# A bank for the first q: attention and two gated layers on one Trainium2 core

## The chip, the core and the metric

The kernel runs on one core of one Trainium2 chip. The metric is device time in microseconds for one launch. The core has a matrix engine (TensorE, PE in the rows, with its weight loads as PEld), a vector engine (VectorE, DVE), a scalar engine (ScalarE, ACT), GpSimd (POOL) and SyncE (SP), which issues most DMAs. Matmuls write into PSUM, which this kernel divides into eight banks of 512 float32 columns.

## The reference

What is computed, cut to what matters: attention over 4 batches, 8 heads, 576 positions and 64 dimensions, in which scores more than tau below their row's maximum are dropped, and behind it two layers with 512 inputs and 2048 hidden values for each of the 2304 tokens.

```python
scores = scale * q @ k.T
thresh = max(scores, axis=-1) - tau
scores = where(scores >= thresh, scores, -1e9)
attn = softmax(scores)            # divided by (sum + 1e-9)
x = (attn @ v), heads side by side, 2304 x 512
h = x @ moe_w_in;  x = (h * clip(h + 3, 0, 6) / 6) @ moe_w_out
h = x @ moe2_w_in; x = (h - tanh(h)) @ moe2_w_out
```

## The kernel before

**Staging.** The work is written as tasks. Each task names its engine, an assumed duration, a key, and the buffers that it reads and writes. Nothing is issued while the tasks are recorded: at the end `plan.issue()` runs a list scheduler over all of them. At each moment, each engine takes, of the tasks whose inputs are ready, the one with the lowest key. The order that comes out is the order in which instructions stand on each engine, so a task that becomes ready at another moment can change the order of all that follows. The chip then runs each engine's instructions in that order, each waiting for its data.

**Buffers.** A `Ring` has n places. For a ring with `free=True`, a task that writes a new buffer can be taken only when one of the places is free, which it is when all users of its last buffer have ended. `R_tp` (L350) is the ring of transposes: two PSUM banks. `R_m` (L397) is layer 1's ring: two banks, too, made for the products of the first layer. One of the two is taken at the start (L980) as `unread`, into which fill-in matmuls write that nobody reads (`filler`, L683): 24 calls' worth before anything else, and further ones wherever PE's planned busy share over the planner's look-back falls under `SHARE`, until the first tokens have been scaled. The other serves the weights of layer 1 in the beginning: `load_w` gets `scratch=R_m` (L1089, L1099), and three VectorE steps (L447, L450, L453) pass each weight through it.

**Attention.** `units` are (batch, half of the rows, pair of heads, head, chunk of 128 rows). For each pair, the rounds come first. `k_round` transposes the keys: part 0 is four PE transposes of the main rows, part 1 two of the left-over 64 rows (L606). Each takes a buffer of `R_tp`; ScalarE copies it (L613) as the high part and VectorE subtracts the high part (L615), which gives the low part, so that the scores can be formed with two products. `q_round` does the same for q: GpSimd doubles the loaded rows (L583), PE makes four transposes (L590), ScalarE copies with the scale (L620) and VectorE subtracts (L622). `v_round` takes a buffer of `R_tp` for a column sum (L657) from which v's scale is made. `softmax` then has PE make the scores (L712), VectorE the maximum (L717), ScalarE the exponential (L719), VectorE the threshold (L728); ScalarE and GpSimd split the result (L733, L739), a DMA transposes it (L742), and `weighted` multiplies it with v (L765).

**Order at the start.** The rounds of a pair have the key `when(u)` of a unit some places ahead: keys six and five units ahead (`LK`), q four (`LQ`), v two (`LV`), with `when(u) = T0 + STEP * u + SLOW * min(u, KNEE)`, T0 8.4, STEP 3.03 and SLOW 0.8. The first pair's first unit is 0, the second pair's is 4. The first q is loaded from ScalarE's queue, all others from SP's. Layer 1 begins when its weights and the first tokens are scaled, and is then interleaved with the attention; the second layer follows, with PE as its bound.

Of the kernel before, what the change touches and what calls it, by code (L numbers as in the profile page):

```python
# [73 lines left out]
class Plan:  # L74
# [13 lines left out]
    def add(self, eng, dur, key, fn, r=(), w=(), after=(), xfer=0.0, hold=False, slack=0.0, port=None):  # L88
        r, w = ([getattr(b, "of", b) for b in x] for x in (r, w))
        deps = dict.fromkeys(after)  # L90
        for b in r:
            deps.update(dict.fromkeys(b.writers))
        t = Task(eng, dur, key, fn, deps, xfer, hold, slack, eng == "pool" if port is None else port)
        t.w = w
        users = dict.fromkeys((*r, *w))
        t.free = [b for b in users if b.ring.free]
        for b in users:
            b.users.append(t)
        for b in w:
            b.writers.append(t)  # L100
        self.tasks.append(t)
        return t
# [110 lines left out]
def attention_moe_moe_kernel(  # L213
# [131 lines left out]
    def at_ring(*a):  # L345
        at_rings.append(ring(*a))
        return at_rings[-1]

    R_s = at_ring(ps_s, 2, [128, 2, 512], F32, "s")
    R_tp = Ring(2, lambda i: ps_t.tile([128, 512], F32, tag=f"tp{i}", name="tp"), free=True)  # L350
# [15 lines left out]
    R_q = at_ring(at_p, 2, [128, 2, 2, 256], F32R, "q")  # L366
# [30 lines left out]
    R_m = Ring(2, lambda i: ps_m.tile([128, 512], F32, tag=f"m{i}", name="m"), free=True)  # L397
# [144 lines left out]
    KR, QR, VR, KL, QL, KS, VT, SV, QT = ({} for _ in range(9))  # L542
# [42 lines left out]
    def transposes(ps, srcs):  # L585

        o = 0
        for s, p0 in srcs:
            w = s.shape[0]
            nc.tensor.transpose(ps[:, o:o + w], s.rearrange("p r d -> p (r d)"), ident[p0:p0 + w, p0:p0 + w])  # L590
            o += w
# [26 lines left out]
    def q_split(qt, tp, out, n, key):  # L618
        src = lambda: tp.t[:, 0:2 * n].rearrange("p (i n) -> p i n", i=2)
        hi = add("act", t_act(2 * n, scalars=True), key + RK, lambda: nc.scalar.activation(  # L620
            out=out(0), in_=src(), func=ACTF.Copy, scale=tau_b[:, 2:3]), r=[tp], w=[qt])
        add("dve", t_dve(2 * n, scalars=True), key + RK, lambda: nc.vector.scalar_tensor_tensor(  # L622
            out=out(1), in0=src(), scalar=tau_b[:, 2:3], in1=out(0).bitcast(F32), op0=ALU.mult, op1=ALU.subtract),
            r=[tp], w=[qt], after=[hi])

    def q_round(b, g, j, key):

        qr, tp, qt = QR[b, g, j], R_tp.new(), R_q.new()
        add("pe", 4 * 0.11, key, lambda: transposes(
            tp.t, [(qr.t[:, i, c, :, :], 0) for i in range(2) for c in range(2)]), r=[qr], w=[tp, qt])  # L630
        q_split(qt, tp, lambda x: qt.t[:, x], 256, key)
        QT[b, g, j] = qt
# [335 lines left out]
    with tc.manual_schedule():  # L968
# [94 lines left out]
        def record_round(r, key):  # L1063
            kind = r[0]
            if kind == "k":
                _, b, j, part = r
                if part == 0:
                    load_k(b, j, key - LD * STEP)
                    if j == 0:
                        load_k_left(b, key - LD * STEP)  # L1070
                k_round(b, j, part, key)
            elif kind == "q":
                _, b, g, j = r
                if g == 1 and 2 * j % NP == 0:
                    load_q_left(b, 2 * j // NP, key - LD * STEP)
                load_q(b, g, j, key - LD * STEP, "act" if (b, g, j) == (0, 0, 0) else "dma")
                q_round(b, g, j, key)
            elif kind == "l":
                q_left_round(r[1], r[2], key)
            elif kind == "v":  # L1080
                load_v(*r[1:], key - LD * STEP)
                v_round(*r[1:], key)
# [410 lines left out]
        for idx, st in enumerate(order2):  # L1493
# [72 lines left out]
            else:  # L1566
                a, b = R_m.new(), R_m.new()
# [55 lines left out]
```

## Time and profile before

| | us |
|---|---|
| median of 3 runs | 1069.54 |
| lowest and highest | 1065.81, 1070.72 |
| the profiled execution | 1068.02 |
| its span in the profile | 1066.2 |
| PE, DVE, ACT, POOL busy | 1011.5, 804.5, 725.0, 362.6 |

The span runs from the first to the last instruction in the profile of one execution. The busy time of PE includes the fill-in matmuls, and the ends of matmuls are modelled. PEclk is the share of TensorE's full clock that was granted; its two levels are 1.2 and 2.4 GHz. "idle before <-releaser" is the time for which an engine stood still before an instruction, and what ended it.

### The profile page before, as it was taken

To read this page: it belongs to the slowest core of one execution; us is meant where nothing else is said; L and a number is where in the kernel's file an instruction comes from. 1 tells how busy PE (TensorE), PEld (TensorE's weight loads), DVE (VectorE), ACT (ScalarE), POOL (GpSimd) and SP (SyncE) were. 2 spreads that over 40 slices of the span, in tenths; PEclk is the share of its full clock that TensorE was granted. 3 is DMA by queue.
4 is the path that set the end of the run, shared out by engine and by line. 5 is a ranking of instruction groups with operands and counts; after the bars stand their busy time and mean duration, and the time that the engine had idled before them with its cause. 6 is when DMAs were issued, how large, how long until landed. Compare 5 with 4: busy or idle time off the path is not lost.

```text
span 1066.2 us, 23814 instructions
## 1 busy us (share of the span) xinstructions
PE 1011.5 (95%) x9202; PEld 775.5 (73%) x9202; DVE 804.5 (75%) x1627; ACT 725.0 (68%) x1345; POOL 362.6 (34%) x385
## 2 busy tenths in 40 slices
PE   7776987899999999999999999999999999999997
PEld 5676776679888778988886778776576666666664
DVE  5999898969887578777457896389976887774573
ACT  7876979889888687877456783468655774664332
POOL 3666667777577455666210000000001111211000
PEclk9999996999999999999999999999999999999999
DMA  7999897767898675876558774143335765664235
GB/s 187 187 228 231 160 228 189 165 133 148 172 189 150 136 147 126 150 160 119 99 163 290 232 210 135 45 150 104 102 122 146 181 140 107 131 118 61 79 108 129
DMA packets 284948, 161.47 MB, mean 151 GB/s; under 512 B 203171, under 2 KB 261027, under 8 KB 284835
## 3 DMA queue, kind: packets, MB, share of 16 engines
q1 hardware_dynamic: 279024, 150.25, 58.1%
q0 software_dynamic: 5184, 9.44, 6.6%
q8 instruction: 72, 1.18, 0.5%
q10 hardware_dynamic: 624, 0.26, 0.1%
q14 instruction: 44, 0.34, 0.1%
HBM read 76.02 MB, written 41.42 MB: 110 GB/s over the span
## 4 chain that ended last, share of the span: by engine, by line
PE 75%; DVE 9%; ACT 7%; DMA 5%; issue 2%; SPq 1%; POOL 0%; DVEq 0%; ACTq 0%; POOLq 0%
PE m L517 22%; PE ya L517 21%; PE h L517 9%; PE m L959 8%; PE s L712 6%; PE tp L765 5%; PE tp L590 2%; DVE e L728 2%; ACT e L719 1%; DVE z L717 1%; DMA pt<-pp 1%; DMA xT<-xs 1%; PE m L686 1%; DVE m L450 1%; ACT pp L733 1%
## 5 line engine op out<-in xcount | busy, mean ns | idle before, releaser
L517 PEld LDWEIGHTS <-wo 128*128 128x128 f16 x2112 | 201.3, 98 | 58.7 <-DVE wo L453 2.2
L739 POOL TENSOR_TENSOR pp<-e,pp 128x128 f16<-128x128 f32 (+3 forms) x156 | 180.5, 1176 | 110.9 <-ACT pp L733 58.8
L517 PE MATMUL ya<-wo,g 128*128 128x512 f16 x864 | 205.4, 379 | 2.5 <-ACT g L879 1.1
L517 PEld LDWEIGHTS <-wi 128*128 128x128 f16 x1536 | 150.0, 98 | 39.3
L517 PE MATMUL m<-xT,wo 128*128 128x256 f16 (+1 forms) x1248 | 170.4, 285 | 2.9 <-DVE wo L453 1.9
L1443 POOL DMA_DIRECT2D po<-o x36 | 31.3, 876 | 410.9 <-ACT o L1437 410.9
L517 PEld LDWEIGHTS <-g 128*128 128x128 f16 x864 | 83.7, 98 | 82.1 <-DVE g L883 3.1
L728 DVE SCALAR_TENSOR_TENSOR e<-s,z,e 128x576 f32<-128x576 f32 x144 | 116.5, 812 | 26.7 <-ACT e L719 23.7
L717 DVE TENSOR_REDUCE z<-s 128x1 f32<-128x576 f32 x144 | 107.4, 750 | 35.4 <-PE s L712 34.4
L959 PE MATMUL m<-g,wo 128*128 128x256 f16 (+1 forms) x960 | 130.8, 284 | 0.7 <-DVE t L873 0.7
L712 PE MATMUL s<-ks,q 128*128 128x288 f32 x512 | 102.3, 324 | 21.9 <-DVE e L728 21.3
L879 ACT ACTIVATE g<-t 128x512 f16<-128x512 f32 (+1 forms) x168 | 94.3, 565 | 37.5 <-DVE t L1410 24.7
L719 ACT ACTIVATE e<-s,z 128x576 f32<-128x576 f32 x144 | 105.0, 737 | 21.8 <-DVE z L717 20.5
L959 PEld LDWEIGHTS <-wo 128*128 128x128 f16 x960 | 88.9, 98 | 21.8 <-DVE t L873 1.0
L712 PEld LDWEIGHTS s<-ks,q 128*128 128x128 f32 x512 | 75.5, 195 | 31.1 <-DVE e L728 13.8
L517 PE MATMUL m<-x,wi 128*128 128x256 f16 x768 | 94.9, 273 | 0.0
L1408 ACT ACTIVATE t<-t,hid_s 128x512 f32<-128x512 f32 x72 | 51.6, 718 | 62.7 <-DVE t L1399 62.2
L733 ACT ACTIVATE pp<-e 128x1152 f16<-128x1152 f32 (+1 forms) x80 | 85.0, 1063 | 12.9 <-DVE e L728 9.9
L765 PE MATMUL tp<-vt,pt 128*128 128x65 f16 (+1 forms) x2240 | 84.2, 196 | 5.6 <-DMA pt<-pp 1.9
L765 PEld LDWEIGHTS <-pt 128*128 128x128 f16 (+1 forms) x2240 | 79.0, 102 | 13.8 <-issue 7.6
L517 PE MATMUL ya<-g,wo 128*128 128x320 f16 (+1 forms) x576 | 77.5, 290 | 0.4 <-DVE g L886 0.2
L871 ACT ACTIVATE t<-m,three,unscale 128x320 f32<-128x320 f32 (+1 forms) x76 | 51.2, 675 | 36.3 <-PE m L517 35.7
(169 smaller groups left out, 1620.3 us busy)
## 6 DMA issues: line engine op xcount, KB each, us to landing
st<-in_moe_w_in_dram SPq DMA_DIRECT2D x32, 512.0 KB, 4.9
st<-in_moe_w_out_dram SPq DMA_DIRECT2D x32, 512.0 KB, 4.7
po<-o POOLq DMA_DIRECT2D x36, 256.0 KB, 4.2
ys<-y SPq DMA_DIRECT2D x32, 160.0 KB, 2.2
y<-ys SPq DMA_DIRECT2D x9, 512.0 KB, 5.8
po<-o SPq DMA_DIRECT2D x18, 256.0 KB, 2.0
o<-po SPq DMA_DIRECT2D x18, 256.0 KB, 3.8
kr<-in_k_dram SPq DMA_DIRECT2D x16, 256.0 KB, 4.2
```

The source lines that it names most:

```text
L517: nc.tensor.matmul(ps, l[a], r[b], start=first and t == 0 and i == 0, stop=last and t == 2 and i == n - 1,)
L712: nc.tensor.matmul(ps.t[:, half, 0:SH], l, ks[:, half * SH:(half + 1) * SH], start=i == 0, stop=i == len(ops) - 1,)
L717: add("dve", 0.69, key, lambda: nc.vector.tensor_reduce(out=z.t[:, 0:1], in_=s(), axis=AX.XY, op=ALU.max, negate=True), r=[ps], w=[z])
L719: exp = add("act", 0.66, key, lambda: nc.scalar.activation(out=ex(), in_=s(), func=ACTF.Exp, bias=z.t[:, 0:1]), r=[ps, z], w=[e])
L728: add("dve", 0.74, key, lambda: nc.vector.scalar_tensor_tensor(out=ex(), in0=s(), scalar=z.t[:, 1:2], in1=ex(), op0=ALU.is_ge, op1=ALU.mul ...
L733: high = add("act", t_act(w * S, sbuf=True), key, lambda: nc.scalar.activation(out=pp.t[:, 0:w, 0:S], in_=e.t[:, 0:w, :], func=ACTF.Copy), ...
L739: add(eng, dur, key, lambda src=src, dst=dst, queue=queue: queue.tensor_tensor(out=pp.t[:, 0:w, dst], in0=e.t[:, 0:w, src], in1=pp.t[:, 0: ...
L765: nc.tensor.matmul(pv.t[0:m, w_ * (D + 1):(w_ + 1) * (D + 1)], pt.t[:, n, blk, rows], vv, start=o == 0, stop=o == len(ops) - 1)
L871: add("act", t_act(n, scalars=True) + 0.05, key, lambda: nc.scalar.activation(out=t(), in_=ps(), func=ACTF.Relu, bias=three[:, 0:1], scale ...
L879: hi = add("act", t_act(n, sbuf=True), key, lambda: nc.scalar.activation(out=gh(), in_=t(), func=ACTF.Copy, scale=GS2 if far else 1.0), r= ...
L959: prev = [add("pe", t_half(n, 1), kd, lambda o=o, l=l, r=r, m=m, s=s, ps=ps, gt=gs[m // 2]: nc.tensor.matmul(ps.t[:, 0:n], W1[half, "o", m ...
L1408: add("act", t_act(2 * NB, sbuf=True, scalars=True), key, lambda: nc.scalar.activation(out=s_(), in_=h.t, func=ACTF.Tanh, scale=c), r=[h], ...
```

## The change

The first q, that of batch 0, first half, first pair of heads, is transposed into a buffer of `R_m` instead of `R_tp`. All other q rounds, the keys and the tasks' durations stay. The order is planned anew by the same scheduler.

```diff
     def q_round(b, g, j, key):
 
-        qr, tp, qt = QR[b, g, j], R_tp.new(), R_q.new()
+        qr, tp, qt = QR[b, g, j], (R_m if (b, g, j) == (0, 0, 0) else R_tp).new(), R_q.new()
         add("pe", 4 * 0.11, key, lambda: transposes(
             tp.t, [(qr.t[:, i, c, :, :], 0) for i in range(2) for c in range(2)]), r=[qr], w=[tp, qt])
         q_split(qt, tp, lambda x: qt.t[:, x], 256, key)
```

## Rows read from the trace of the kernel before

**Rows 1.** The page: the span and the busy time of each engine.
```profile
span 1066.2 us, 23814 instructions
...
PE 1011.5 (95%) x9202; PEld 775.5 (73%) x9202; DVE 804.5 (75%) x1627; ACT 725.0 (68%) x1345; POOL 362.6 (34%) x385
```
**Rows 2.** Busy time by stretch: stretch, length, engines (instructions), granted clock, DMA share, GB/s.
```profile
20.00:240.00 220.00, 180.23 (x2029) 152.02 (x2028) 197.71 (x390) 183.42 (x339) 150.75 (x158) 0.94 0.84 187
240.00:1066.00 826.00, 816.32 (x7087) 612.07 (x7085) 597.13 (x1211) 529.38 (x985) 207.94 (x210) 1.00 0.60 140
```
**Rows 3.** PE in order of time, 5 to 15 us: start, length, line, operation.
```profile
5.51 1.06 PE L590 MATMUL tp<-ident,kr 128*128 128x128 f32 x4
6.50 0.35 PE L606 MATMUL tp<-ident,left 64*64 64x64 f32 x2
6.78 0.75 PE L686 MATMUL m<-ones 128*128 128x224 bf16 x6
9.48 0.63 PE L590 MATMUL tp<-ident,qr 128*128 128x128 f32 x4 [1.95 <-DVE ks L615]
9.95 0.32 PE L657 MATMUL tp<-vs,ones 128*128 128x1 f32 x2
10.13 1.66 PE L686 MATMUL m<-ones 128*128 128x224 bf16 x8
11.58 1.06 PE L590 MATMUL tp<-ident,kr 128*128 128x128 f32 x4
12.57 0.42 PE L606 MATMUL tp<-ident,left 64*64 64x64 f32 x2
12.92 1.57 PE L712 MATMUL s<-ks,q 128*128 128x288 f32 x8
```
**Rows 4.** GpSimd in order of time: the first q is doubled.
```profile
5.42 0.40 POOL L583 COPY qr<-qr 128x256 f32<-128x256 f32 x1 [3.71 <-DMA qr<-in_q_dram]
```
**Rows 5.** VectorE in order of time, 7 to 37 us, and the weights' entries at L447.
```profile
7.84 1.71 DVE L615 TENSOR_TENSOR ks<-tp,ks 64x512 fp32r<-64x512 f32 x3 [3.41 <-ACT ks L613]
...
10.87 0.75 DVE L622 SCALAR_TENSOR_TENSOR q<-tp,tau_b,q 128x512 fp32r<-128x512 f32 x1
13.91 1.39 DVE L615 TENSOR_TENSOR ks<-tp,ks 64x512 fp32r<-64x512 f32 x2 [2.29 <-ACT ks L613]
15.33 0.76 DVE L717 TENSOR_REDUCE z<-s 128x1 f32<-128x576 f32 x1
...
18.21 0.68 DVE L447 TENSOR_SCALAR m<-wo 128x512 int32<-128x512 int32 x1
...
30.65 0.69 DVE L447 TENSOR_SCALAR m<-wo 128x512 int32<-128x512 int32 x1
...
36.06 0.68 DVE L447 TENSOR_SCALAR m<-wo 128x512 int32<-128x512 int32 x1
```
**Rows 6.** ScalarE in order of time, 6 to 14 us.
```profile
6.61 1.49 ACT L613 ACTIVATE ks<-tp 64x512 fp32r<-64x512 f32 x3 [3.57 <-PE tp L590]
8.00 0.73 ACT L655 ACTIVATE vt<-vr 128x640 f16<-128x640 f32 x1
...
10.15 0.69 ACT L620 ACTIVATE q<-tp,tau_b 128x512 fp32r<-128x512 f32 x1 [1.33 <-PE tp L590]
...
12.68 1.20 ACT L613 ACTIVATE ks<-tp 64x512 fp32r<-64x512 f32 x2 [0.90 <-PE tp L590]
```
**Rows 7.** DMA issues between 4.4 and 5.0 us: size, median us to landing.
```profile
kr<-in_k_dram SPq DMA_DIRECT2D x1, 256.0 KB, 3.8
```
**Rows 8.** Busy time by stretch, two stretches of 2 us, columns as in rows 2.
```profile
10.00:12.00 2.00, 2.00 (x14) 1.75 (x13) 1.23 (x4) 1.51 (x2) 0.00 (x0) 0.51 0.98 326
22.00:24.00 2.00, 1.54 (x15) 1.32 (x14) 1.67 (x3) 1.99 (x4) 1.72 (x3) 1.00 0.00 1
```
**Rows 9.** The chain that ended last, its longest piece between 20 and 60 us.
```profile
35.91 5.45 DMA st<-in_moe_w_in_dram
```
**Rows 10.** Busy time by stretch, columns as in rows 2.
```profile
165.00:185.00 20.00, 15.13 (x130) 12.18 (x130) 16.61 (x41) 18.50 (x34) 16.17 (x17) 0.57 0.73 170
```

## The prediction

> **What bounds the kernel now.** I read the page first, then its forty slices cut coarser with the view of busy time by stretch, then the first 36 us engine by engine in order of time, and last the chain that ended last. The page says that PE is busy for 1011.5 of 1066.2 us [rows 1]. That figure hides two regimes. From 240 us on PE is busy for 816.32 of 826 us at a granted clock of 1.00, so this part has a length of its own and only its start can move. From 20 to 240 us PE is busy for 180.23 of 220 us, part of it fill-in matmuls that nobody reads, while VectorE works 197.71 us and ScalarE 183.42 us [rows 2]. There the softmax and the preparation of layer 1's weights set the pace through VectorE and ScalarE, and PE waits for them. So the change has to be judged by one question: how much earlier do VectorE and ScalarE get their first full queue, and does that lead survive until 240 us?
>
> In the opening PE's order is: four key transposes (5.51), two left-over key transposes (6.50), six fill-in matmuls (6.78), then an idle 1.95 us ended by VectorE's ks, then the first q (9.48), the column sum of v (9.95), eight fill-ins (10.13), the second pair's keys (11.58) and their rest (12.57), and the first two score units (12.92) [rows 3]. The q data is ready long before: GpSimd has doubled it by 5.42 + 0.40 = 5.82 us [rows 4]. What it waits for is the bank: the two banks of transposes hold the two key rounds until VectorE has subtracted out of them, and the first of the two comes free shortly before 9.48, behind the second of the three subtractions that fill 7.84 to 9.55 [rows 5]. That is the wait that the change takes away.
>
> **The change part by part.** Removed: q's use of one of the two transpose banks. Added: q's use of one of layer 1's two banks. No instruction, byte or DMA is added or dropped; the fill-in matmuls, which the planner puts in where PE looks idle, may change in number, and the list planner writes out a new order for every engine.
>
> Is the other bank free? One of layer 1's two is held by the fill-in matmuls from the start. The other is first written by VectorE when it prepares a weight, L447 at 18.21 [rows 5]. Since q is out of the bank near 10.3 us (below), there are about 8 us between the two, and I cost this edit at nothing; without that cover it would cost the weight's start the overlap.
>
> Where does q land in PE's order? The keys in the source give -14.6 and -10.8 for the two key rounds, -6.9 for q and 0.7 for the second pair's keys and for v (T0 + STEP*u + SLOW*u with u = -6, -5, -4, -2). So q comes third, right behind the left-over keys, before any fill-in. I use the planner only for this order; the times are the trace's.
>
> PE: the left-over keys end at 6.50 + 0.35 = 6.85, q takes 0.63, so it ends at 7.48 instead of 10.11 [rows 3]. ScalarE: its three ks copies end at 6.61 + 1.49 = 8.10; q's copy takes 0.69, to 8.79 instead of 10.84; the absolute sum of v, 0.73 with its read-out to 8.82 now, slides behind it to about 9.6 [rows 6]. VectorE: its three subtractions end at 7.84 + 1.71 = 9.55; q's takes 0.75, to 10.30 instead of 10.87 + 0.75 = 11.62 [rows 5]. So q itself is complete 1.3 us earlier.
>
> The second gain is what q leaves behind. The first transpose bank, free shortly before 9.48, no longer goes to q, so the second pair's keys can take it. Their data was issued at about 4.43 and landed 3.8 us later, near 8.2 [rows 7], so they start where q starts today, 9.48, instead of 11.58: 2.1 us earlier. Two things between fall out of the path, q's 0.63 and the eight fill-ins' 1.66 [rows 3]. v's column sum goes behind these keys, to about 10.6, some 0.6 us later than now; it feeds v's scaling, whose result is first needed by the weighted sums. This step I cost at nothing because by the source a weighted sum stands behind the softmax, its split and a transposing DMA; without that cover it would be 0.6 us.
>
> Following the second keys with the distances of today: ScalarE takes them 1.10 us after their start (12.68 against 11.58), so at 10.6, when it has been free since 9.6; VectorE takes them 2.33 us after their start (13.91), so at 11.8, when it has been free since q at 10.3 or, with v's small scale, 11.4; the first maximum, L717, stands behind their 1.39 us, 15.33 now, so 13.2 [rows 3, 5, 6]. The first two score units, 1.57 us [rows 3], now can start near 10.9 and would be done at 12.5; they stay covered by the key subtractions. This is the sum: the first softmax starts 15.33 - 13.2 = 2.1 us earlier.
>
> Here the clock has to be weighed. In 10 to 12 us the granted clock is 0.51, the lower level of 1.2 GHz, behind the idle PE of 7.5 to 9.5 us [rows 8]. The new order leaves nearly the same gap (7.48 to 9.48), so I expect the same fall, and the key transposes that I moved keep their price, as the 1.06 us were run in that stretch. The scores move into it: if they took twice as long, the first unit's half of 1.57 us would end at 10.9 + 1.57 = 12.5, still before 13.2. Cost nothing; if the cover were gone, 0.8 us. The Trainium skill, "TensorE: Matmul & The Clock Gate", section "What's actually happening", says that the throttled clock is the default and that activity releases it. By that rule the fill-ins that drop out speak against this change, since they are activity; the sum would then be 2.1 - 0.8 = 1.3 us.
>
> Bounds of the head start: 1.3 us from below, where the second keys gain no more than q does; 2.6 us from above, the whole 9.48 - 6.85 by which q moves. I take 2.1 us, the value of the row that feeds VectorE.
>
> Does it last? VectorE and ScalarE are nearly full from 14 us on, and in 20 to 240 us their work is fixed, so a queue that starts 2.1 us earlier should hand over 2.1 us earlier. DMA does not stand in the way at first: in 22 to 24 us its share is 0.00 because all load buffers are full [rows 8]. Against it: VectorE has 22 us without work in 20 to 240, and the chain goes through a weight load of 5.45 us at 35.91 [rows 9]. That load waits for a buffer that VectorE frees, so it should move along, but what else is on the queue then may not. From below nothing lasts (0), from above all of 2.6 us; I take the whole 2.1 because the stretch behind is paced by the engines that start earlier.
>
> Sum: 1066.2 - 2.1 = 1064.1 us of span. The profiled execution took 1068.02 us, 1.8 more than its span, which makes 1065.9; the median of the runs, 1069.54, stands 1.5 above that execution, so I predict 1067.4 us, 0.2% faster. Half a per cent, 5.3 us, is about what a measurement of this kernel can tell from no change (its runs lie between 1065.81 and 1070.72), so this counts as the same.
>
> **The rivals.** *The lead is absorbed, or is not there.* Some load or ring later in the first 240 us sets its own time, or the planner lets q wait for something else. For it: the 22 us that VectorE idles, the load in the chain [rows 2, 9]. Against it: the loads' buffers are freed by the same engines. Time: 1069.5.
>
> *A better hand: a stretch at the lower clock falls out.* The new order is dealt again for all that follows. In 165 to 185 us PE is busy 15.13 us at a granted clock of 0.57 [rows 10]; at 1.00 the same work takes 15.13 x 0.57 = 8.6, so 6.5 us could be won where that work is on the path. For it: PE is nearly full soon after. Against it: ScalarE is busy for 18.50 and VectorE for 16.61 of these 20 us, so PE's work is largely not what the stretch waits for. Time: 1067.4 - 6.5 = 1060.9, faster by 0.8%.
>
> *The weights slip on layer 1's one open bank.* Place: VectorE's L447, L450, L453, which pass each weight of layer 1 through the very bank that q now borrows, one weight at a time. Successive weights enter it at 18.21, 30.65 and 36.06 [rows 5]. If the attention's tasks, ready earlier, get in front and the chain of weights falls back by a place, layer 1's first pass starts one interval later, 36.06 - 30.65 = 5.4 us. Against 2.1 us of head start one interval gives 1072.8, 0.3% slower; it decides from two intervals on, 10.8 us: 1078.2, slower by 0.8%. For it: softmax and weights share VectorE, which has little to spare. Against it: q is out of the bank 8 us before the first weight, and the keys are unchanged, so a late weight is soon the one with the lowest key.
>
> **How the numbers follow.** The head start that lasts: 0.50, 1066 to 1069 us. Absorbed or absent: 0.24, about 1069.5. A better hand: 0.14, about 1061. The weights slip by two places or more: 0.12, from 1075 to 1080 (a slip by one place, 1072.8, is held with the first two). Those are within 0.5% of 1069.54 (1064.2 to 1074.9), so faster is 0.14, same 0.74, slower 0.12. For the range, leaving out half of the better hand (0.07) and the two-interval end of the slip (0.10) leaves 0.83 between 1061 and 1075. The likeliest case's own range, from 2.6 us of lead to 0, is 1066.9 to 1069.5, and with the spread of the runs 1065 to 1070.
>
> **What would show it.** Right: q's transposes stand before 7.6 us, directly behind the left-over keys; the second keys start near 9.5; the first L717 near 13.2 instead of 15.33; the stretch from 240 us on has the same busy time and starts about 2 us earlier. Wrong: q still behind 9 us (the change does nothing), the first L717 early but the first matmuls of layer 1 and the sum of PE in 20 to 240 us unchanged (absorbed), L447's entries later than 18.21, 30.65 and 36.06 (slip), or another row for 165 to 185 us with a granted clock near 1.00 (better hand). The prediction fails as a size if the new order changes the useful work that PE has done by 240 us by more than some 5 us either way.

## The result, and the profile after

| | before | after |
|---|---|---|
| median, us (6 runs each) | 1069.97 | 1082.24 |
| lowest and highest | 1065.81, 1070.72 | 1080.48, 1084.77 |
| the profiled execution | 1068.02 | 1080.48 |
| its span | 1066.2 | 1078.7 |

The ratio after to before is 1.0112, interval [1.0095, 1.0128]: the change makes the kernel 1.1% slower. The forecast was 1067.4 us in a range of 1061 to 1075, so the prediction is wrong, in sign and in size.

**The opening went as foreseen.** PE of the kernel after, in order of time (start, length, line, operation, idle time before and what ended it):

```profile
5.51 0.74 PE L590 MATMUL tp<-ident,kr 128*128 128x128 f32 x4
6.46 0.30 PE L606 MATMUL tp<-ident,left 64*64 64x64 f32 x2 [0.20 <-DMA left<-in_k_dram]
6.68 0.66 PE L590 MATMUL m<-ident,qr 128*128 128x128 f32 x4
9.01 0.92 PE L590 MATMUL tp<-ident,kr 128*128 128x128 f32 x4 [1.67 <-DVE ks L615]
9.87 0.42 PE L606 MATMUL tp<-ident,left 64*64 64x64 f32 x2
10.22 0.93 PE L686 MATMUL m<-ones 128*128 128x224 bf16 x4
10.83 2.11 PE L712 MATMUL s<-ks,q 128*128 128x288 f32 x8
12.77 0.32 PE L657 MATMUL tp<-vs,ones 128*128 128x1 f32 x2
...
81.22 0.64 PE L590 MATMUL tp<-ident,kr 128*128 128x128 f32 x4
81.78 0.30 PE L606 MATMUL tp<-ident,left 64*64 64x64 f32 x2
...
105.53 0.27 PE L497 MATMUL tp<-ident,xtop 128*1 128x128 f32 x1
...
113.10 1.75 PE L765 MATMUL tp<-vt,pt 128*128 128x65 f16 x28
115.30 0.63 PE L853 MATMUL tp<-ident,x 128*128 128x128 f32 x4 [0.46 <-ACT x L772]
117.89 0.63 PE L853 MATMUL tp<-ident,x 128*128 128x128 f32 x4 [1.95 <-DVE xT L858]
120.62 3.36 PE L765 MATMUL tp<-vt,pt 128*64 128x65 f16 x56 [2.11 <-DVE xT L858]
...
124.68 1.54 PE L517 MATMUL m<-xT,wo 128*128 128x256 f16 x10
```

The first eight lines answer to [rows 3]: q stands third, at 6.68 instead of 9.48, and the second pair's keys follow at 9.01 instead of 11.58. VectorE of the kernel after, in the same view, answers to [rows 5]:

```profile
11.90 1.01 DVE L615 TENSOR_TENSOR ks<-tp,ks 64x512 fp32r<-64x512 f32 x2
12.94 0.76 DVE L717 TENSOR_REDUCE z<-s 128x1 f32<-128x576 f32 x1
...
101.24 0.69 DVE L615 TENSOR_TENSOR ks<-tp,ks 64x512 fp32r<-64x512 f32 x1
...
104.79 0.69 DVE L615 TENSOR_TENSOR ks<-tp,ks 64x512 fp32r<-64x512 f32 x1
...
120.72 0.28 DVE L615 TENSOR_TENSOR ks<-tp,ks 64x128 fp32r<-64x128 f32 x1
```

The first maximum, L717, starts at 12.94 instead of 15.33: a head start of 2.4 us, which the next units keep (the 17th L717 starts at 59.8, before at 62.6; by the 36th, at 150.5 against 140.6, it is gone and 9.9 us are lost).

**The lead is lost between 80 and 140 us, and far more with it.** Busy time of the kernel after by stretch (stretch, length, PE, PEld, VectorE, ScalarE, GpSimd busy with instructions, granted clock, DMA share, GB/s):

```profile
80.00:140.00 60.00, 45.26 (x475) 40.39 (x472) 48.53 (x97) 43.31 (x78) 33.40 (x36) 0.86 0.71 160
...
165.00:185.00 20.00, 9.85 (x115) 8.58 (x114) 16.02 (x37) 19.00 (x38) 16.41 (x16) 0.79 0.88 213
...
20.00:240.00 220.00, 174.33 (x1951) 147.84 (x1951) 189.37 (x370) 175.71 (x321) 143.97 (x150) 0.91 0.84 184
240.00:1078.70 838.70, 827.77 (x7189) 620.19 (x7185) 603.92 (x1228) 538.15 (x1002) 214.59 (x217) 1.00 0.58 139
```

The first of these stretches in the kernel before, and the one from 140 to 210 us, which is used further below:

```profile
80.00:140.00 60.00, 48.47 (x581) 42.15 (x580) 55.38 (x109) 50.31 (x91) 39.56 (x44) 0.97 0.86 194
140.00:210.00 70.00, 56.89 (x571) 45.93 (x570) 64.86 (x138) 60.14 (x110) 49.73 (x52) 0.85 0.84 196
```

In these 60 us VectorE does 48.53 us of work instead of 55.38, that is 6.85 less; over 20 to 240 us it does 189.37 instead of 197.71 [rows 2], 8.34 less. So most of what it falls behind, it falls behind here. Cut finer, VectorE is level with before until 120 us (36.32 us of work from 80 to 120, before 35.95); ScalarE falls behind from 100 to 120, VectorE from 120 to 140. The two stretches before and then after:

```profile
100.00:120.00 20.00, 16.14 (x208) 14.19 (x208) 16.64 (x36) 17.11 (x30) 11.48 (x14) 1.00 1.04 213
120.00:140.00 20.00, 18.66 (x231) 16.34 (x230) 19.44 (x37) 18.86 (x35) 15.11 (x15) 1.00 0.66 137
```

```profile
100.00:120.00 20.00, 11.89 (x116) 9.99 (x117) 18.32 (x39) 10.94 (x19) 5.24 (x7) 0.88 0.42 112
120.00:140.00 20.00, 19.38 (x231) 17.59 (x231) 12.21 (x24) 15.95 (x30) 13.05 (x14) 0.87 0.90 174
```

What is not done by 240 us has to be done later, where PE has no room: PE has 827.77 us left instead of 816.32 [rows 2]. These 11.45 us are nearly all of the 12.5 us by which the span grew. The kernel from 240 us on is as tight as before (granted clock 1.00); it only got more work handed over.

The place where it looks jammed: the keys of batch 1's first pair are transposed at 81.22 and 81.78, long before they are needed (before transposes the main ones at 114.49), and take both transpose banks. VectorE subtracts out of the one at 101.24 and 104.79 and out of the other at 120.72. In between the first tokens' scale (L497) gets its turn at 105.53 (97.88 before) and weighted sums and token transposes (L765, L853) pass one by one, each waiting for a read-out. Layer 1's first matmul, L517, comes at 124.68 instead of 108.06, 16.6 us late. The weight load of L497 names the subtraction that frees the first bank, and VectorE's longest wait between 20 and 240 us comes right after the second subtraction, for a q that PE transposed at 123.79:

```profile
105.53 0.08 PEld L497 LDWEIGHTS tp<-ident,xtop 128*1 128x1 f32 x1 [0.22 <-DVE ks L615]
...
125.65 0.75 DVE L622 SCALAR_TENSOR_TENSOR q<-tp,tau_b,q 128x512 fp32r<-128x512 f32 x1 [4.64 <-ACT q L620]
```

The jam looks like the cause. Whether it is, the experiments have to say.

### The profile page after: what moved, and what is told of

Same layout as the page of the kernel before. It is cut to its first block, busy times and chain, and to the rows that moved or that the text cites. A ratio compares the mean times of both kernels' runs of the same rounds, so it can differ in the third digit from the quotient of the medians.

```text
span 1078.7 us, 23879 instructions
## 1 busy us (share of the span) xinstructions
PE 1017.2 (94%) x9228; PEld 779.9 (72%) x9228; DVE 804.7 (75%) x1627; ACT 726.5 (67%) x1345; POOL 363.3 (34%) x385
## 4 chain that ended last, share of the span: by engine, by line
PE 76%; DVE 11%; ACT 5%; DMA 4%; issue 2%; SPq 1%; POOL 1%; DVEq 0%; POOLq 0%; ACTq 0%
PE ya L517 22%; PE m L517 20%; PE m L959 10%; PE h L517 8%; PE s L712 6%; PE tp L765 5%; DVE e L728 2%; DVE z L717 2%; DMA pt<-pp 2%; PE tp L590 1%; DVE wo L453 1%; DVE m L450 1%; ACT e L719 1%; DVE m L447 1%; DVE ks L615 1%
## 5 line engine op out<-in xcount | busy, mean ns | idle before, releaser
L517 PEld LDWEIGHTS <-wo 128*128 128x128 f16 x2112 | 200.7, 98 | 56.1 <-issue 1.4
L517 PE MATMUL ya<-wo,g 128*128 128x512 f16 x864 | 205.4, 379 | 2.5 <-DVE g L883 1.3
L517 PEld LDWEIGHTS <-wi 128*128 128x128 f16 x1536 | 150.0, 98 | 39.3
L517 PE MATMUL m<-xT,wo 128*128 128x256 f16 (+1 forms) x1248 | 171.2, 286 | 0.6 <-DVE t L873 0.3
L517 PEld LDWEIGHTS <-g 128*128 128x128 f16 x864 | 83.7, 98 | 82.1 <-DVE g L883 3.1
L717 DVE TENSOR_REDUCE z<-s 128x1 f32<-128x576 f32 x144 | 107.7, 751 | 33.2 <-PE s L712 32.3
L712 PE MATMUL s<-ks,q 128*128 128x288 f32 x512 | 101.9, 324 | 19.9 <-DVE e L728 14.8
L712 PEld LDWEIGHTS s<-ks,q 128*128 128x128 f32 x512 | 75.5, 196 | 28.9 <-issue 15.6
L765 PE MATMUL tp<-vt,pt 128*128 128x65 f16 (+1 forms) x2240 | 86.2, 198 | 10.8 <-DVE ks L615 5.0
L517 PE MATMUL m<-x,wi 128*128 128x256 f16 x768 | 94.9, 273 | 0.0
L765 PEld LDWEIGHTS <-pt 128*128 128x128 f16 (+1 forms) x2240 | 80.6, 103 | 19.5 <-issue 13.9
L517 PE MATMUL ya<-g,wo 128*128 128x320 f16 (+1 forms) x576 | 77.5, 290 | 0.1
```

What stands on the lines that cost most here:

```text
L517: nc.tensor.matmul(ps, l[a], r[b], start=first and t == 0 and i == 0, stop=last and t == 2 and i == n - 1,)
L712: nc.tensor.matmul(ps.t[:, half, 0:SH], l, ks[:, half * SH:(half + 1) * SH], start=i == 0, stop=i == len(ops) - 1,)
L717: add("dve", 0.69, key, lambda: nc.vector.tensor_reduce(out=z.t[:, 0:1], in_=s(), axis=AX.XY, op=ALU.max, negate=True), r=[ps], w=[z])
L765: nc.tensor.matmul(pv.t[0:m, w_ * (D + 1):(w_ + 1) * (D + 1)], pt.t[:, n, blk, rows], vv, start=o == 0, stop=o == len(ops) - 1)
```

## The experiments

**How they are made.** `plan.issue()` is split in two, without touching the scheduler: `simulate()` plans and leaves a list of tasks in the order of issue, `emit(log)` issues such a list. So the buffer for which the planner plans and the one which the kernel uses can differ, and the list can be edited by hand. In e3, e5 and e6 the list is issued as planned. The snippets below are cut to what differs, in short names. Where a helper adds lines, line numbers shift; the text gives the name of before. Each ratio is against the kernel before on the same chip.

| run | median, us | before on that chip | ratio, interval | first L717 | first L517 | PE left at 240 us |
|---|---|---|---|---|---|---|
| before | 1069.97 | | | 15.33 | 108.1 | 816.32 |
| after | 1082.24 | 1069.97 | 1.0112 [1.0095, 1.0128] | 12.94 | 124.7 | 827.77 |
| e1_bank | 1070.36 | 1071.01 | 0.9995 [0.9980, 1.0011] | 13.73 | 107.7 | 818.35 |
| e2_order | 1084.41 | 1071.01 | 1.0125 [1.0108, 1.0142] | 15.58 | 127.6 | 830.73 |
| e3_hold | 1080.81 | 1071.01 | 1.0093 [1.0071, 1.0114] | 12.93 | 101.7 | 826.61 |
| e4_lead | 1068.05 | 1071.01 | 0.9977 [0.9962, 0.9992] | 11.93 | 104.1 | 814.41 |
| e5_fill22 | 1087.30 | 1071.42 | 1.0158 [1.0129, 1.0186] | 13.17 | 111.6 | 833.97 |
| e6_m_fill26 | 1073.14 | 1071.42 | 1.0016 [0.9993, 1.0039] | 13.33 | 114.1 | 822.32 |
| e7_no_fill | 1070.68 | single run | | 12.54 | 107.4 | 818.13 |
| e8_split_early | 1081.37 | 1071.42 | 1.0101 [1.0070, 1.0132] | 11.96 | 124.1 | 828.14 |
| e9_fill_early | 1070.12 | 1069.69 | 1.0008 [0.9990, 1.0027] | 14.09 | 107.6 | 815.61 |
| e10_no_fill_timed | 1068.17 | 1069.69 | 0.9988 [0.9969, 1.0008] | 12.62 | 108.7 | 818.84 |
| e11_lead_again | 1067.10 | 1069.69 | 0.9972 [0.9957, 0.9987] | 12.49 | 106.2 | 815.09 |

The last three columns are start times and the busy time of PE from 240 us to the end, from the one profiled execution of each. Executions differ: e4 and e11 are the same kernel, e7 and e10 are too, and after and e8 have the same opening, and yet their first L717 lie 0.56, 0.08 and 0.98 us apart. So a difference of a microsecond in these columns says nothing by itself.

### Bank or order: e1 and e2

The change does two things: it puts q into another bank, and it makes the planner write another order. e1 keeps before's order and moves only the bank; e2 takes after's order and leaves q in a transpose bank.

```diff
 # e1: planned with R_tp, issued with the place of R_m that no fill-in uses
+plan.simulate()
+FIRST_Q.ring, FIRST_Q.slot = R_m, 1
+plan.emit(plan.log)
 # e2: planned with R_m, issued with R_tp; the few tasks of the opening
 # that need it are put behind q's read-out
+plan.simulate()
+FIRST_Q.ring, FIRST_Q.slot = R_tp, 0
+plan.emit(EDIT(plan.log))
```

> The instructions of the kernel before in its own order on every engine; only the first q's transposes go to layer 1's second bank. Theory A (the new order costs, the bank does not): same as before, 1068 to 1072 us. Theory B (the bank itself costs, through fill-in matmuls beside it or the weights behind it): most of the 12 us, 1078 to 1083. First L717 of VectorE at 15.3 us, as before, by both.

> The other half: the changed kernel's order on every engine, but the first q's transposes stay in the ring of transposes, so they must wait for its bank. Theory A (order): 1081 to 1086 us, the opening some 2 us later than in the changed kernel. Theory B (bank): back to 1068 to 1073.

PE's work left at 240 us in e1 and in e2, columns as above:

```profile
240.00:1071.10 831.10, 818.35 (x7097) 612.68 (x7096) 598.47 (x1213) 530.75 (x989) 209.39 (x210) 1.00 0.59 140
```

```profile
240.00:1081.80 841.80, 830.73 (x7229) 621.96 (x7226) 605.26 (x1230) 541.29 (x1006) 217.09 (x219) 1.00 0.58 139
```

e1 is the same as before (0.9995), e2 is as slow as after (1.0125), although its first maximum starts at 15.58, without any head start, and q is back in its old bank. So the bank is not what costs, and the head start is not what costs either: the whole loss comes with the order. e1 also shows a head start that cannot be seen in the time: its first L717 is 1.6 us early (13.73; 15.3 was expected), which would be 0.9985 if it lasted; the interval holds that as well as no gain. How much of the 1.6 us is q's was not separated: in the profiled execution of e1 the granted clock was 1.00 in 10 to 12 us, in that of before 0.51 [rows 8]. e1 bears, too, on the rival in which weights slip on layer 1's open bank: q lies in that very bank and nothing is lost.

### Is it the two held transpose banks: e3 and e8

e3 plans after's kernel once more, with one more dependence: the keys of batch 1's first pair may not be transposed before the first tokens' scale is there. This ends the hold of both banks in 81 to 121 us, but deals a new order. A bank is still held by keys: in e3 one from 104.46 to 120.87 us, in the kernel before one from 76.23 to 97.15 and one from 114.49 to 123.75. e8 keeps after's order and takes only the jam out of it: the three ScalarE copies and three VectorE subtractions of these keys stand right behind their transposes, and later transposes use the two banks in turn.

```diff
 # e3
+for p in range(2):
+    keys[1, 0, p].deps[scaled[0, 0]] = None
 # e8, on the list that the planner of after left
+splits = [t for t in users_of(keys[1, 0]) if t is not a transpose]   # six
+log = up_to(keys[1, 0, 1]) + splits + the rest without splits
```

> The changed kernel, planned anew with one constraint: the transposes of the keys of batch 1's first pair wait until the first tokens are scaled, so they cannot sit in both transpose banks from 81 to 121 us. Theory A1 (this hold is the loss): the first matmul of layer 1 near 105 us instead of 124.7 and 1066 to 1071 us. Theory A2 (any newly dealt order loses about as much, at another place): the first matmul of layer 1 early, 95 to 108 us, and still 1076 to 1084.

> The changed kernel's own order, with one edit by hand: ScalarE's and VectorE's splits of the keys that hold the two transpose banks from 81 us are moved to right behind these transposes, and the buffers behind them use the two banks in turn. Nothing else moves. If the held banks make the hole at 100 to 125 us, the first matmul of layer 1 comes 5 to 12 us earlier than 124.7 and the time falls to 1071 to 1078 us. If PE's order makes it, the first matmul of layer 1 stays within 3 us of 124.7 and the time at 1080 to 1084.

PE in e3 and in e8 around the start of layer 1 (the helper shifts L517 to L543 in e3, and L497, L517 and L712 to L537, L557 and L758 in e8):

```profile
101.72 2.94 PE L543 MATMUL m<-xT,wo 128*128 128x256 f16 x12 [0.78 <-ACT xT L888]
```

```profile
106.74 0.76 PE L758 MATMUL s<-ks,q 128*128 128x288 f32 x4 [0.81 <-DVE z L771]
107.34 0.27 PE L537 MATMUL tp<-ident,xtop 128*1 128x128 f32 x1
...
124.07 2.34 PE L557 MATMUL m<-xT,wo 128*128 128x256 f16 x10
```

VectorE in e8, the subtractions of those keys (L615, here L657), and the stretches from 120 to 140 us and from 240 us on:

```profile
83.14 0.68 DVE L657 TENSOR_TENSOR ks<-tp,ks 64x512 fp32r<-64x512 f32 x1 [0.16 <-ACT ks L655]
84.49 0.99 DVE L657 TENSOR_TENSOR ks<-tp,ks 64x512 fp32r<-64x512 f32 x2 [0.66 <-ACT ks L655]
```

```profile
120.00:140.00 20.00, 17.81 (x201) 15.63 (x201) 12.61 (x25) 16.45 (x31) 13.83 (x15) 0.91 0.99 178
240.00:1080.60 840.60, 828.14 (x7198) 620.36 (x7194) 604.04 (x1229) 538.47 (x1002) 214.79 (x217) 1.00 0.58 139
```

In e8 both banks are free by 85.5 us instead of 121, and yet L497 starts at 107.34, later than after's 105.53, and L517 at 124.07. The bank that the trace named at 105.53 was only the last of what L497 waited for. In the written order scores stand right before L497, and in e8 they wait for VectorE (106.74). VectorE's shortfall in 120 to 140 us is there as in after, 12.61 against 12.21. PE's work left is 828.14 us, the time 1.0101: nothing is won.

e3 removes the late start of layer 1 altogether (101.72, even 6.3 us before the kernel before) and is still 0.9% slower. Busy time of e3 by stretch shows where the loss went:

```profile
80.00:140.00 60.00, 48.19 (x505) 41.29 (x502) 53.02 (x103) 47.43 (x86) 37.51 (x39) 0.86 0.80 178
140.00:210.00 70.00, 52.62 (x483) 43.85 (x480) 60.90 (x128) 57.20 (x104) 48.91 (x51) 0.76 0.79 192
```

VectorE lost 2.4 us against before in the first of these stretches and, with 60.90 against 64.86, 4.0 us in the second. The 36th L717 is on time at 140.2 (140.6 before), the 52nd late, at 210.1 against 198.3. So the theory that the two held banks are the cause falls: without both held at once, in either way, the kernel is as slow; and e6 below, which is not slow, holds one of them for the same keys from 90.41 to 118.61 us. It was a good reading of one wait, and wrong as an explanation of the 12 us.

### Does any new deal cost: e5 and e6

If the order as a whole is what differs, a re-deal that has nothing to do with q should move the time as well. e5 is the kernel before with two fill-in matmuls fewer at the start (22 instead of 24: the constant counts matmuls, not calls; the trace shows x22); e6 is the kernel after with two more. A new deal, here, is an order that the planner writes anew.

```diff
-SHARE, FC, FIRST_FILL = 0.51, 224, 24
+SHARE, FC, FIRST_FILL = 0.51, 224, 22     # e5, on before
+SHARE, FC, FIRST_FILL = 0.51, 224, 26     # e6, on after
```

> The kernel before with the first q in the ring of transposes, and one constant changed: 22 fill-in calls at the start instead of 24, which by itself frees PE some 0.4 us earlier. Everything is planned anew. If the loss came with the borrowed bank, this is the same as before, 1068 to 1072 us. If any newly dealt order costs (the order of before is a good draw among such orders), it is slower without any change of banks: 1074 to 1082.

> The changed kernel, first q in layer 1's bank, with 26 fill-in calls at the start instead of 24, planned anew. If the borrowed bank makes the order bad in general, it stays slow, 1079 to 1085 us. If the changed kernel's order is one poor draw among many, another draw with the same bank lands elsewhere: 1068 to 1076.

From 240 us on, e5 and e6:

```profile
240.00:1086.20 846.20, 833.97 (x7235) 624.77 (x7233) 604.47 (x1224) 537.86 (x999) 214.22 (x216) 1.00 0.57 138
```

```profile
240.00:1071.80 831.80, 822.32 (x7126) 615.91 (x7125) 601.99 (x1216) 532.25 (x990) 210.39 (x211) 1.00 0.58 140
```

e5 moves no bank and loses 1.6%, more than the change under study and more than was expected of it. e6 has q in layer 1's bank, as after, and is not to be told from before (1.0016, interval over 1). Four orders were dealt anew by the planner (after, e3, e5, e6): 1.1, 0.9, 1.6 and 0.2% more than before (the last not clear of the noise), none less. That suits an order of before that is a good one among many; four deals cannot show it. Which it is follows from none of the three edits in a way that I could read beforehand. What it does follow, in all runs, is PE's work left at 240 us: 814 to 816 go with 1067 to 1070 us, 818 with 1068 to 1071, 822 with 1073, 827 to 828 with 1081 to 1082, 831 with 1084, 834 with 1087. PE is full from there on, so this number says when the time was lost, before 240 us, and not why.

### What the early q is worth by itself: e4, e11, e9

e4 takes before's order as the planner left it and rearranges only the opening by hand, in the way that the prediction described: q behind the left-over keys, the second pair's keys in the bank that it leaves; and, beyond the change, fourteen fill-in matmuls between q and those keys, and the two key rounds' splits where they come soonest. Everything behind the opening stands as in before, with the two transpose banks exchanged. e11 is e4 again, with more runs. e9 moves only the eight fill-ins ahead of q, and leaves q in its old bank.

```diff
 # e4 and e11, on the list that the planner of before left; q in R_m as in e1
+order = [k0, k0_rest, Q, FILL * 7, k1, v_sum, k1_rest, scores, ...]   # PE
+# ScalarE, VectorE: splits of q behind those of k0, splits of k1 ahead of v's scale
+for b in later buffers of R_tp: b.slot = 1 - b.slot
 # e9
+order = [k0, k0_rest, FILL * 7, Q, v_sum, k1, ...]                    # PE
```

> The order of the kernel before on every engine, but for the opening by hand: the first q goes to layer 1's bank right behind the left-over keys, the second pair's keys follow it, then v's column sum; all fourteen fill-ins stand between q and those keys. Theory L1 (a lead of some 2 us lasts where the later order is kept): first L717 near 13 us, 1066.5 to 1068.5. Theory L2 (the lead is absorbed by later waits): first L717 near 13 us, but 1069 to 1071.

> The order of the kernel before on every engine, first q in the ring of transposes as before; only the eight fill-in matmuls that stood between v's column sum and the second keys move ahead of q, into PE's idle time. It asks how much of the hand-made opening's gain comes from the fill-ins alone. If all: 1067 to 1069 us and first L717 near 12 us. If q's own place matters: first L717 near 13.5 us and a ratio of 0.999 to 1.000.

> The hand-made opening with its fill-ins once more, beside the two others on the same chip: a ratio of 0.996 to 0.999, first L717 near 12 us.

PE of e4 in order of time (L621 is L590, L637 is L606, L722 is L686, L748 is L712):

```profile
5.93 0.30 PE L637 MATMUL tp<-ident,left 64*64 64x64 f32 x2
6.16 0.66 PE L621 MATMUL m<-ident,qr 128*128 128x128 f32 x4
6.65 1.50 PE L722 MATMUL m<-ones 128*128 128x224 bf16 x14
8.62 0.63 PE L621 MATMUL tp<-ident,kr 128*128 128x128 f32 x4 [0.46 <-DVE ks L647]
...
9.96 1.32 PE L748 MATMUL s<-ks,q 128*128 128x288 f32 x8
```

The stretch from 240 us on of e4, and of e11:

```profile
240.00:1066.80 826.80, 814.41 (x7072) 609.72 (x7071) 596.50 (x1210) 527.58 (x981) 206.32 (x208) 1.00 0.59 140
```

```profile
240.00:1065.70 825.70, 815.09 (x7081) 611.13 (x7078) 597.42 (x1211) 528.97 (x983) 207.54 (x209) 1.00 0.60 140
```

With the order behind it kept, the hand-made opening wins: 0.9977 and 0.9972, both intervals below 1, in medians 3.0 and 2.6 us. PE's work left is 1.9 and 1.2 us less than before [rows 2], which is within what one execution differs from another. This is the version that beats both kernels. The fill-ins alone (e9, 1.0008) and q's other bank alone (e1, 0.9995) give nothing that shows. How much of the gain is that of q's early place, of the second keys' bank, of the splits put in another order or of the fill-ins was not separated.

### What the clock takes: e7 and e10

e7 is e4 without the fourteen fill-ins between q and the second keys; e10 is the same kernel timed, beside e11.

```diff
-order = [k0, k0_rest, Q, FILL * 7, k1, ...]
+order = [k0, k0_rest, Q, k1, ...]
```

> The hand-made opening on the order of before, without the fourteen fill-in matmuls behind the first q; one look for the clock. By the prediction's step the lower clock then stays behind the key subtractions and costs nothing: granted clock near 0.5 in 10 to 12 us, first L717 within 0.3 us of the same opening with fill-ins. If the clock does count, the first L717 comes 0.8 us or more later than there.

> The hand-made opening without its fourteen fill-ins again, now timed. If the lower clock of 10 to 16 us costs nothing behind the key subtractions, as the prediction had it: the same ratio as with fill-ins, 0.996 to 0.999. If it costs, as the single look hints (first softmax 0.6 us later, unit 36 some 3 us later): 1.000 to 1.002.

Busy time by stretch, e4 and e7, 10 to 12 us; the last three columns are granted clock, DMA share, GB/s:

```profile
10.00:12.00 2.00, 1.28 (x9) 1.05 (x8) 1.51 (x4) 1.94 (x3) 0.00 (x0) 1.00 1.00 323
```

```profile
10.00:12.00 2.00, 1.75 (x8) 1.51 (x8) 1.35 (x5) 1.93 (x4) 0.00 (x0) 0.50 1.02 342
```

Without the fill-ins TensorE is granted 0.50, the lower level, in all of 10 to 16 us; with them 1.00; e10 and e11, the same two kernels once more, show the same. The first L717 is 0.6 us later in e7 than in e4 (12.54 and 11.93), between what the two theories expected, and the 36th 3.3 us later (140.6 and 137.3). But e10 and e11 make it 0.13 us (12.62 and 12.49) and 2.1 us (141.9 and 139.8), and at the 17th e10 is the earlier one (61.3 and 61.5); e4 and e11, one kernel, lie 2.5 us apart at the 36th. So these starts give the clock no price. In the time e10 stands 1.1 us above e11, 0.9988 [0.9969, 1.0008] against 0.9972 [0.9957, 0.9987]. The intervals overlap, so the clock's price for the whole kernel lies between nothing and some 0.3% and stays undecided. Fill-ins are not all that decides the clock there: in e1 no fill-in is moved, and e8 has after's opening, and yet their profiled executions show 1.00 in 10 to 14 us.

## Why the prediction was wrong, step by step

**What bounds the kernel: right.** From 240 us on all kernels run PE at 1.00 with 9 to 13 us without work, and the time is set by what is left over at that point. The question that the prediction put, whether the lead survives until 240 us, was the right one.

**The opening: right, with one miss.** Forecast: q ends at 7.48, second keys at 9.48, first L717 at 13.2. Measured: 6.68 + 0.66 = 7.34, 9.01 and 12.94. The miss is v's column sum, forecast near 10.6: it came at 12.77, since the second pair's left-over keys took the other transpose bank at 9.87, ahead of it, a task that I had not put in the row for that bank. What this costs was not tried by itself; VectorE takes v's small scale behind the first maximum, and the lead at the 17th unit is still there. That L717 came within 0.3 us of the forecast is luck in part: e8, with the same opening, has it at 11.96.

**The clock in the opening: right, for the place where it was costed.** After has 0.50 in 10 to 12 us (0.51 before, [rows 8]), and the first scores take 2.11 us instead of 1.57 [rows 3], but VectorE's subtractions run until 11.90 + 1.01 = 12.91 and L717 starts at 12.94. So they stay covered, as the prediction said. The rule in the Trainium skill, "TensorE: Matmul & The Clock Gate", section "What's actually happening", that activity is what releases the throttle, agrees with e4 against e7 (1.00 and 0.50 in 10 to 12 us). The forecast of the same fall behind the same gap holds for the profiled execution of after and not for that of e8, whose clock, with the same opening, is 1.00 until 14 us.

**"I take the whole 2.1 because the stretch behind is paced by the engines that start earlier": this is the step that failed.** The term for what lasts until 240 us was +2.1 us; it measured 816.32 - 827.77 = -11.45 us. The reason is in the clause before it, "in 20 to 240 us their work is fixed, so a queue that starts 2.1 us earlier should hand over 2.1 us earlier". The sum of work is fixed, the queue is not. The planner deals every engine's order anew once one task becomes ready at another time, and VectorE, with 22 us of slack in that stretch, gets less done by its end: in the four new deals 8.3 (after), 7.0 (e3), 4.9 (e5) and 6.1 us (e6) less than before. Where the order behind the opening is held, the runs fit a lead that lasts: e4 and e11 have the first L717 3.4 and 2.8 us early (11.93 and 12.49) and keep 3.0 and 2.6 us in the medians. They do not prove it: e10 has it 2.7 us early and, like e1 with 1.6 us, is not clear of before. So the prediction computed what an early q is worth, and not what the change does.

**The rivals.** *Absorbed* did not happen. *A better hand* treated the re-deal as something that can only win, and only in one place. That place did change, to a granted clock of 0.79 with 9.85 us of PE work in 165 to 185 us, from 0.57 with 15.13 [rows 10]. But the lower clock did not fall out, it came later. 180 to 200 us in before and in after:

```profile
180.00:200.00 20.00, 16.99 (x128) 12.64 (x128) 17.16 (x34) 18.31 (x34) 15.38 (x17) 0.90 0.73 177
```

```profile
180.00:200.00 20.00, 14.38 (x120) 11.49 (x121) 15.16 (x35) 17.21 (x32) 12.69 (x13) 0.66 0.57 136
```

So this rival's condition was never met, and what such a stretch is worth stays open.

*The weights slip* had the right side: the 16th L453 starts at 103.2 instead of 100.2 and the 32nd at 225.7 instead of 216.8. But its sign failed: the first three entries at L447 come earlier, at 16.35, 21.77 and 34.55, not later than 18.21, 30.65 and 36.06 [rows 5]. That q's stay in layer 1's open bank costs by itself is excluded by e1. That attention tasks get in front of weights, the other half of this rival, is part of the new order, and no run tried it alone.

**The chances.** A re-deal had 0.14 on the good side, and on the bad side only the 0.12 of a single mechanism, with the range cut off at 1075. Yet the text's own last sentence names the outcome: PE's useful work done by 240 us changes by more than 5 us. The view of busy time gave a size for this beforehand: VectorE's 22.3 us without work in 20 to 240 us [rows 2]. Had I taken half of that as what a worse deal may add, the range would have reached 1080, still short of 1082.24. An order that the planner has never dealt should be given a width of its own, to both sides.

**What stays open.** Which property of an order makes it hand over 816 or 834 us at 240 us. It is not the held transpose banks alone (e3, e8), nor the start of layer 1 (e3 starts it earliest of all and is slow; e6 starts it 6 us late and is not), nor the head start (e2 has none and is as slow as after). One sign goes with it: in 120 to 140 us VectorE is busy for 18.9 us or more in every run within 0.3% of before (19.44 in before itself, 19.21 in e6), and for 12.2 to 17.0 us in the five slow ones (12.21 in after, 12.53 in e2, 12.61 in e8, 14.19 in e5, 16.97 in e3). Whether that is the cause or one more symptom, no run tried.

## What to carry to other kernels

Where a scheduler writes the order, a change to one buffer is two changes: the wait that it removes and a new order for all that follows. Cost them apart, and run them apart: the old order with the new buffer, and the new order with the old buffer, took two runs here and settled it. And where a gain in the opening is real (0.23 to 0.28% for the hand-made one here), take it by editing the order in place, or by comparing several deals, and not by what one new deal happens to bring; a wait that stands out in the trace of a slower deal may be its symptom, and is worth an experiment before it is called the cause.

## What the runs showed of the hardware

A wait's named releaser can be the last of several and worth nothing: L497 started 0.05 us after "DVE ks L615" had ended (104.79 + 0.69 = 105.48), and with that bank free 20 us earlier it started 1.8 us later (e8). With fill-in matmuls of 1.50 us in the opening the granted clock was 1.00 from 6 to 16 us (e4, e11), without them 0.50 from 10 to 16 us (e7, e10), and in 12 runs each that difference could hardly be told in the whole (1067.10 and 1068.17 us). The granted clock also differed between two executions with the same opening: 0.50 in 10 to 12 us in after, 1.00 in e8.
